# Loading `wq` as two 64-row transfers, one issued by SyncE and one by ScalarE

## The chip, the cores and the metric

The kernel runs on one core of a Trainium2 chip. The metric is the device time of one execution in microseconds. The kernel before took 680.11 us (median of three runs, 680.04 to 680.23). One execution was profiled; numbers of instructions, transfers and waits below come from it.

## The reference

Eight batch rows of one decode step: a layer norm of `x`, grouped-query attention over a cached K and V of 4096 positions, and a gated MLP whose SiLU gates the attention output. Cut to what matters:

```python
# x [8,1,512], k_cache and v_cache [8,8,4096,128], wq [512,4096], wo [4096,512]
xn = layernorm(x)
q = (xn @ wq) as [8, 32 heads, 1, 128]            # 4 query heads share one of the 8 KV heads
p = softmax(q @ k^T * 128**-0.5);  o = p @ v
s = o as [8,1,4096] @ wo
z = gelu(xn @ w_in); z1, z2 = halves of 896; z2 = layernorm(z2)
g = silu((z1 * (w_sp * z2 + b_sp)) @ w_out)
out = x + s * g
```

All data are float32. K and V are 134.2 MB each, so nearly all of the bytes are the cache.

## The kernel before, in words

Everything that is large is staged through a ring of three SBUF slots (`ring`, line 68; `slot()`, line 75). A slot has 128 rows (partitions) of 16384 float32, that is 64 KB a row and 8.39 MB in all. The loads go round the ring in program order, and each is issued by SyncE with one `dma_start` of 128 rows:

- slot 0: `wq` (line 80), the weight of the query projection, laid out as 4 blocks of 4096 columns a row;
- slot 1: `mlp_slot`, which holds `x` (line 96; 8 rows of 2 KB), `w_mlp` (line 97; 128 rows of 39 KB: `w_in`, most of `w_out`, the side constants) and the four `w_ex` pieces (line 101; rows of `w_out` that are fetched separately to 12 or 20 rows). The first `w_ex` waits for a memset by GpSimd (line 99);
- slots 2, 0, 1, 2, 0, 1, ...: for each of the 8 KV heads two halves of K (`load_k`, line 318) and two halves of V (`load_v`, line 323), 32 loads of 8.39 MB;
- after the last of them, `wo` in six pieces (line 365) in one more slot, and `x_rows` (line 367).

So the second K half of head 0 goes into the slot that `wq` had, and the first V half into the slot of the MLP weights. A load is issued when its slot has been read for the last time; SyncE's queue is in order, so a load that waits holds up all loads behind it.

Besides the slot, a load waits for the semaphore on which it will tell of its landing: there are eight of them for DMAs, taken in turn by all loads in program order. The load that takes a semaphore a second time waits until the load that had it eight places before has landed.

The compute of the head of the kernel runs in this order: the layer norm (lines 145 to 149, 8 rows of VectorE work and a power on GpSimd), its transpose `xnT` (line 152), two query projections of 32 matmul records each (`project_q`, line 247, which read `wq_sb`), and the MLP (`mlp()`, lines 157 to 240), whose last reads of the MLP slot are the matmuls of lines 223 and 227. Then, head after head, `scores` (line 267), `softmax` (lines 270 to 296) and `values` (line 303). At the end `project_o` (line 341) and `direct` (line 386) multiply by `wo`, two VectorE operations (lines 404 and 405) apply the gate and add `x`, and ScalarE issues the store (line 406).

ScalarE otherwise has little to do: its first instruction in the kernel before is the table load for the `Tanh` of the MLP (line 178).

Of the kernel before, what the change touches and what calls it, by code (L numbers as in the profile page):

```python
# [13 lines left out]
P = 128  # L14
# [46 lines left out]
def tile_gqa_gmlp_decode(ctx: ExitStack, tc: tile.TileContext, x, kT, v, wq, wo, w_mlp, w_ex0, w_ex1, w_ex2, w_ex3, x_rows, out, gate, stored):  # L61
    nc = tc.nc
# [12 lines left out]
    def slot():  # L75
        return ring.tile([P, SLOT], F32, name="slot")


    wq_sb = slot()
    nc.sync.dma_start(wq_sb, wq)  # L80
    wq_sb = wq_sb.rearrange("p (k n) -> p k n", k=NK)
    mlp_slot = slot()
    n_in, n_out = NK * 2 * FH, (NB - MOVED) * D
# [376 lines left out]
```

## Time and profile before

| | |
|---|---|
| median of 3 runs | 680.11 us |
| the profiled execution | 680.09 us |
| its span, first to last instruction | 678.5 us |
| mean granted clock of TensorE | 0.748 |
| TensorE matmul busy | 342.9 us (51% of the span) |
| VectorE / ScalarE / GpSimd busy | 81.2 / 13.8 / 7.9 us |
| read from HBM | 290.78 MB, 429 GB/s over the span |

How to read it: the page gives the busy time of each engine, then the span in 40 equal slices with a digit for the busy share in tenths, the mean share of the 16 DMA engines and the GB/s that they moved. The chain of waits follows the work that ended last back from the last instruction. A name such as "SPq" is an engine's sequencer, which issues DMAs and waits; "PE" is TensorE, "DVE" VectorE, "ACT" ScalarE, "POOL" GpSimd, "SP" SyncE. A window's GB/s counts a DMA packet where it starts; in this kernel a packet is one row of a transfer.

### The profile page before, as it was taken

To read this page: it belongs to the slowest core of one execution; us is meant where nothing else is said; L and a number is where in the kernel's file an instruction comes from. 1 tells how busy PE (TensorE), PEld (TensorE's weight loads), DVE (VectorE), ACT (ScalarE), POOL (GpSimd) and SP (SyncE) were. 2 spreads that over 40 slices of the span, in tenths; PEclk is the share of its full clock that TensorE was granted. 3 is DMA by queue.
4 is the path that set the end of the run, shared out by engine and by line. 5 is a ranking of instruction groups with operands and counts; after the bars stand their busy time and mean duration, and the time that the engine had idled before them with its cause. 6 is when DMAs were issued, how large, how long until landed. Compare 5 with 4: busy or idle time off the path is not lost.

```text
span 678.5 us, 5312 instructions
## 1 busy us (share of the span) xinstructions
PE 342.9 (51%) x2465; PEld 94.4 (14%) x2465; DVE 81.2 (12%) x155; ACT 13.8 (2%) x28; POOL 7.9 (1%) x17
## 2 busy tenths in 40 slices
PE   0448744346555444555553444555544346555547
PEld 0112211111111111111111011111111011111103
DVE  1143021102100021101101021101111021100211
ACT  0010000000000000000000000000000000000000
POOL 3000000000000000000000000000000000000000
PEclk9987856787766678787666778777656777876669
DMA  9999999999999999999999999999999999999997
GB/s 379 458 440 430 430 433 430 433 430 433 430 437 430 433 433 430 437 430 437 434 433 441 440 433 430 433 430 440 434 437 430 433 433 430 430 437 437 434 428 300
DMA packets 6165, 291.15 MB, mean 429 GB/s; under 512 B 952, under 2 KB 1080, under 8 KB 1496
## 3 DMA queue, kind: packets, MB, share of 16 engines
q1 hardware_dynamic: 6000, 290.79, 99.2%
q8 instruction: 19, 0.31, 0.2%
q10 hardware_dynamic: 144, 0.03, 0.0%
q14 instruction: 2, 0.02, 0.0%
HBM read 290.78 MB, written 0.03 MB: 429 GB/s over the span
## 4 chain that ended last, share of the span: by engine, by line
DMA 78%; PE 16%; issue 4%; DVE 0%; SPq 0%; POOLq 0%; POOL 0%
DMA slot<-in_kT 35%; DMA slot<-in_v 33%; PE sc L267 7%; PE o_ps L303 7%; DMA slot<-in_wo 7%; DMA slot<-in_x 3%; PE scr L223 1%; PE scr L227 1%; SPq L365 0%; PE acc L386 0%; PE scr L216 0%; DVE st L145 0%; POOLq L454 0%; POOL rstd L148 0%; PE scr L205 0%
## 5 line engine op out<-in xcount | busy, mean ns | idle before, releaser
L267 PE MATMUL sc<-slot,qz 128*32 128x512 f32 x1024 | 146.2, 735 | 129.9 <-DMA slot<-in_kT 129.9
L303 PE MATMUL o_ps<-slot,pT 128*16 128x512 f32 x1024 | 147.6, 741 | 112.1 <-DMA slot<-in_v 112.1
L267 PEld LDWEIGHTS sc<-slot,qz 128*32 128x32 f32 x1024 | 38.3, 132 | 231.2 <-issue 149.6
L303 PEld LDWEIGHTS o_ps<-slot,pT 128*16 128x16 f32 x1024 | 32.9, 113 | 213.6 <-issue 151.2
L272 DVE TENSOR_REDUCE nm<-sc 128x1 f32<-128x1024 f32 x8 | 9.8, 1225 | 273.2 <-PE sc L267 273.2
L306 DVE TENSOR_TENSOR o_all<-o_ps,diag 128x512 f32<-128x512 f32 x16 | 11.1, 692 | 245.9 <-PE o_ps L303 245.9
L313 PE MATMUL po_ps<-fold,o_sb 128*128 128x16 f32 x32 | 6.4, 276 | 28.4 <-DVE o_sb L308 28.4
L274 ACT ACTIVATE p<-sc,nm 128x1024 f32<-128x1024 f32 x8 | 8.9, 1113 | 551.6 <-DVE nm L272 551.6
L308 DVE TENSOR_REDUCE o_sb<-o_all 128x128 f32<-128x512 f32 x16 | 16.7, 1045 | 0.5
L152 PE MATMUL scr<-ident,slot 8*128 8x8 f32 x4 | 0.6, 254 | 25.1 <-DVE slot L149 25.1
L313 PEld LDWEIGHTS po_ps<-fold,o_sb 128*128 128x128 f32 x32 | 4.9, 190 | 42.7 <-DVE o_sb L308 42.3
L294 DVE STREAM_TRANSPOSE pT<-p 128x1024 f32<-128x1024 f32 x8 | 10.0, 1245 | 0.3
L247 PE MATMUL scr<-slot,xnT 128*32 128x512 f32 x64 | 9.2, 726 | 0.3 <-issue 0.3
L277 PE MATMUL scr<-ident,nm 128*1 128x128 f32 x8 | 2.2, 270 | 10.8 <-DVE nm L272 10.8
L290 PE MATMUL scr<-wl,same 128*128 128x1 f32 x16 | 3.8, 309 | 6.5 <-DVE wl L288 6.5
L292 DVE TENSOR_SCALAR p<-p,w,wl 128x1024 f32<-128x1024 f32 x8 | 6.5, 813 | 0.3
L341 PE MATMUL sc<-slot,oT 128*8 128x256 f32 x56 | 5.0, 380 | 1.6 <-DMA slot<-in_wo 1.6
L223 PE MATMUL scr<-slot,rest 128*32 128x512 f32 x10 | 5.5, 1057 | 0.0
L186 PE MATMUL scr<-part_sum,same 128*128 128x1 f32 x4 | 1.1, 347 | 8.4 <-DVE part_sum L184 8.4
L341 PE MATMUL o_ps<-slot,oT 128*8 128x256 f32 x56 | 4.8, 379 | 0.0
L290 PEld LDWEIGHTS scr<-wl,same 128*128 128x128 f32 x16 | 3.4, 265 | 7.0 <-PE scr L283 7.0
L283 PE MATMUL scr<-ident,full 1*128 1x1 f32 x8 | 1.8, 226 | 5.1 <-DVE full L281 5.1
(93 smaller groups left out, 69.5 us busy)
## 6 DMA issues: line engine op xcount, KB each, us to landing
slot<-in_w_mlp SPq DMA_DIRECT2D x1, 4880.0 KB, 32.6
slot<-in_wo SPq DMA_DIRECT2D x1, 4608.0 KB, 39.5
slot<-in_wo SPq DMA_DIRECT2D x1, 2048.0 KB, 44.0
slot<-in_wo SPq DMA_DIRECT2D x2, 512.0 KB, 44.8
slot<-in_wo SPq DMA_DIRECT2D x1, 384.0 KB
slot<-in_kT SPq DMA_DIRECT2D x16, 48.5
slot<-in_v SPq DMA_DIRECT2D x16, 48.3
slot<-in_w_ex SPq DMA_DIRECT2D x1, 240.0 KB
```

The costliest lines, as they stand in the source:

```text
L223: nc.tensor.matmul(pw[R * g:R * (g + 1), :], hT[:, a, R * g:R * (g + 1)], w_out_sb[:, i, :], start=(a == 0), stop=False)
L247: nc.tensor.matmul(pq[R * g:R * (g + 1), :], xnT[:, k, :], wq_sb[:, k, lo:lo + REP * DH], start=(k == 0), stop=(k == NK - 1))
L267: nc.tensor.matmul(sc[R * g:R * (g + 1), c, :], qz[:, h, b * R:(b + 1) * R], k_sb[:, i, c, g, :], start=(b == 0), stop=(b == B - 1))
L272: nc.vector.tensor_reduce(m, sc, op=ALU.max, axis=AX.XY, negate=True)
L274: nc.scalar.activation(p, sc.rearrange("p c s -> p (c s)"), AF.Exp, bias=m, accum_out=l[:, h:h + 1])
L290: nc.tensor.matmul(tot, same_all, wl, start=True, stop=True)
L294: nc.vector.transpose(pT.rearrange("p j b g r -> p j g b r"), p.rearrange("p (j g b r) -> p j g b r", j=J, g=G, b=B))
L303: nc.tensor.matmul(of[R * i:R * i + G * REP, :], pT[:, j, half * HALF + i], v_sb[:, i, j], start=(j == 0), stop=(j == J - 1))
L306: nc.vector.tensor_mul(o_all, o, diag[:, :, None].to_broadcast([P, G, DH]))
L308: nc.vector.tensor_reduce(o_sb, o_all.rearrange("p g d -> p d g"), op=ALU.add, axis=AX.X)
L313: nc.tensor.matmul(po[:, half * n:(half + 1) * n], o_sb, fold.rearrange("p i r -> p (i r)"), start=True, stop=True)
L341: mm = nc.tensor.matmul(part[i][R * q:R * q + B, :], oT[:, h, r, :], wo_sb[:, m, i * half_d:(i + 1) * half_d], start=(m < REP), stop=(m == ...
```

## The change

One line is replaced by two. Rows 0 to 63 of `wq` are loaded by SyncE, at the place in its queue where all 128 rows were; rows 64 to 127 are loaded by ScalarE, as the first DMA of its queue and its first instruction. The bytes, the source, the destination and the length of a row (64 KB) are the same.

```diff
     wq_sb = slot()
-    nc.sync.dma_start(wq_sb, wq)
+    nc.sync.dma_start(wq_sb[:P // 2], wq[:P // 2])
+    nc.scalar.dma_start(wq_sb[P // 2:], wq[P // 2:])
     wq_sb = wq_sb.rearrange("p (k n) -> p k n", k=NK)
```

There is one DMA more, so every later load takes the next semaphore of the eight. Lines of the changed kernel from the second `dma_start` on have numbers higher by one.

In the instruction streams as built, the order on every engine is otherwise as before. The first matmul of `project_q` waits for the semaphores of both halves. The first K load, which waited for nothing before, is now the ninth DMA and waits for the semaphore of SyncE's half of `wq`; the second K load waits for that of ScalarE's half and for TensorE, where before it waited for that of the whole `wq` and for TensorE.

## The prediction

> **What bounds the kernel now.** I read the page's slices first, then the queues, then the chain of waits.
>
> ```profile
> span 678.5 us, 5312 instructions
> DMA  9999999999999999999999999999999999999997
> GB/s 379 458 440 430 430 433 430 433 430 433 430 437 430 433 433 430 437 430 437 434 433 441 440 433 430 433 430 440 434 437 430 433 433 430 430 437 437 434 428 300
> ...
> q1 hardware_dynamic: 6000, 290.79, 99.2%
> ...
> DMA 78%; PE 16%; issue 4%; DVE 0%; SPq 0%; POOLq 0%; POOL 0%
> ```
>
> The DMA engines are busy in every slice, at 430 to 440 GB/s; one queue, SyncE's, carries 290.79 MB; 78% of the chain is DMA. The rest of the chain is matmuls, so the question is whether any transfer waits for them. In the chain, in order of time (start, length, what):
>
> ```profile
> 1.16 21.61 DMA slot<-in_x
> ...
> 60.82 3.59 PE scr L227 x14
> ...
> 64.47 31.83 DMA slot<-in_v
> ...
> 96.43 9.65 PE o_ps L303 x64
> ...
> 106.09 48.11 DMA slot<-in_kT
> ...
> 570.00 47.85 DMA slot<-in_kT
> ...
> 630.03 44.75 DMA slot<-in_wo
> ```
>
> A K load is issued at 106.09, when its slot is free, and lands 48.1 us later; the last K of the chain lands at 570.00 + 47.85 = 617.85. From the landing of the first V (64.47 + 31.83 = 96.30) to there lie 9 turns of the chain, each one turn of the three-slot ring, so 27 loads: 521.55 / 27 = 19.32 us a load, and 8.39 MB in 19.32 us is 434 GB/s. A load that takes 48 us to land after its issue therefore stands behind about 29 us of other transfers: the queue never runs dry, and the ten microseconds of matmuls in the chain delay nothing. The windows by stage say the same (stretch, length, busy time of each engine, TensorE clock, DMA share, GB/s):
>
> ```profile
> 0.00:23.00 23.00, 0.00 (x0) 0.00 (x0) 2.09 (x8) 0.00 (x0) 6.75 (x15) 1.00 0.94 393
> 23.00:35.00 12.00, 8.75 (x60) 2.99 (x64) 2.49 (x7) 0.00 (x0) 0.54 (x1) 1.00 1.02 443
> ...
> 96.00:640.00 544.00, 274.75 (x1864) 71.83 (x1868) 55.48 (x91) 9.85 (x21) 0.00 (x0) 0.72 1.00 434
> ```
>
> So the time is one stream of DMAs, plus a start of under 2 us and a tail. A microsecond that the stream loses anywhere is a microsecond of the kernel, and one that compute gains in the head is worth nothing.
>
> **The head.** SyncE's issues, the first work of ScalarE, and how the compute stands to them:
>
> ```profile
> 0.73 0.37 SPq L80 DMA_DIRECT2D slot<-in_wq  x1
> 1.16 0.35 SPq L96 DMA_DIRECT2D slot<-in_x  x1
> 1.55 0.35 SPq L97 DMA_DIRECT2D slot<-in_w_mlp  x1
> 3.98 3.25 SPq L101 DMA_DIRECT2D slot<-in_w_ex  x4
> 7.27 29.73 SPq L318 DMA_DIRECT2D slot<-in_kT  x2
> 64.47 8.39 SPq L323 DMA_DIRECT2D slot<-in_v  x2
> ...
> 44.53 1.28 ACT L178 ACT_TABLE_LOAD   x1 [44.53 <-DVE zu L177]
> ```
>
> ```profile
> 22.79 0.68 DVE L145 BATCH_NORM_STATS2 st<-slot 8x6 f32<-8x512 f32 x1 [17.68 <-DMA slot<-in_x]
> ...
> 26.02 5.55 PE L247 MATMUL scr<-slot,xnT 128*32 128x512 f32 x32 [0.33 <-issue]
> ...
> 77.03 5.34 PE L267 MATMUL sc<-slot,qz 128*32 128x512 f32 x32 [4.54 <-DMA slot<-in_kT]
> ...
> slot<-in_w_mlp SPq DMA_DIRECT2D x1, 4880.0 KB, 32.6
> slot<-in_wq SPq DMA_DIRECT2D x1, 21.9
> ```
>
> `wq` lands at 0.73 + 21.9 = 22.6, `x` right behind it, `w_mlp` at 1.55 + 32.6 = 34.2. The second K is issued at about 36.7, while the first K is under way, and lands just before 77.03; the first V is issued at 64.47, so at that moment the stream still has 12.5 us of work.
>
> **The change part by part.** *Issue.* SyncE's issue of 64 rows is bounded by nothing and by the 0.37 us that it took for 128; the two issues behind it keep their places. ScalarE's new issue is priced at the same 0.37 us and stands where ScalarE idles until 44.53; without that cover it would cost 0.37 us once. If both sequencers share what makes the packets, the stream might start up to 0.37 us later or earlier: plus or minus 0.4, taken as 0.
>
> *Waits.* TensorE's first `project_q` matmul waits for two semaphores instead of one; the row at 26.02 shows 0.33 us of idling there, which bounds it, and it lies off the stream: 0. The first K load, issued at 7.27 before, now waits until SyncE's half of `wq` has landed. Behind it on SyncE wait the second K and the first V, and TensorE waits for those. What covers it are the transfers of `w_mlp` and `w_ex`, which stand behind that half in SyncE's own queue: 34.2 - 22.6 = 11.6 us for `w_mlp` alone, against an issue of 0.37 and a start of under 1 us (1.16 to the first rows at 1.50 to 2.25, below). Cost 0, with some 10 us to spare; with no cover it would be a hole of about 1.5 us.
>
> *The transfer.* The bytes and the rows stay, so a fair sharing of the 16 engines costs nothing. That is the lower end: 0. The upper end comes from how the engines move rows now (windows of 0.75 us, with the empty stretches between them):
>
> ```profile
> 1.50:2.25 0.75, 0.00 (x0) 0.00 (x0) 0.48 (x1) 0.00 (x0) 0.75 (x1) 1.00 4.25 1398
> 2.25:4.50 2.25, 0.00 (x0) 0.00 (x0) 0.18 (x1) 0.00 (x0) 2.21 (x5) 1.00 0.00 0
> ...
> 14.25:15.00 0.75, 0.00 (x0) 0.00 (x0) 0.00 (x0) 0.00 (x0) 0.00 (x0) 1.00 3.22 1398
> 15.00:16.75 1.75, 0.00 (x0) 0.00 (x0) 0.00 (x0) 0.00 (x0) 0.00 (x0) 1.00 0.00 0
> 16.75:17.50 0.75, 0.00 (x0) 0.00 (x0) 0.00 (x0) 0.00 (x0) 0.00 (x0) 1.00 3.23 1398
> 17.50:19.25 1.75, 0.00 (x0) 0.00 (x0) 0.00 (x0) 0.00 (x0) 0.00 (x0) 1.00 0.00 0
> 19.25:20.00 0.75, 0.00 (x0) 0.00 (x0) 0.00 (x0) 0.00 (x0) 0.00 (x0) 1.00 3.23 1398
> ```
>
> 1398 GB/s in 0.75 us is 1.05 MB, exactly sixteen rows of 65,536 bytes: each engine starts one row, then none starts for 1.75 us, then sixteen again. The engines take whole rows, one at a time, and march in step; a step is 19.32 / 8 = 2.42 us. Now let the ways into SBUF belong to the rows rather than to the engines. With 128 rows in one transfer each engine has eight rows and a way of its own. With 64 rows spread over the same 16 engines, the engines would stand two to a way. Each row then takes two steps, 4.83 us. The other queue's half uses the other ways, but because the engines march in step and take the queues in turn, all would write low rows, then all high rows, and half of the ways would idle at any moment. Each half takes what a whole slot takes now: 2 x 19.32 = 38.64 instead of 19.32, a loss of 19.3 us.
>
> No row of this trace has two engines on one way, or 64 rows, so the price lies between 0 and 19.3. I take the side of the upper end, since the windows show the lockstep that it needs: a steady 434 GB/s with all engines starting within 0.75 us after eight rows says that nothing shuffles them apart. A pair that is offset by some time saves that offset at each of the 7 row changes. Sixteen starts fit in 0.75 us at every step, so an offset within a pair is between 0 and 0.75, a saving of 0 to 5.3; I take 0.2 us, 1.4 in all, as the starts must fill the window between them and a pair is two of sixteen. The loss is then 19.3 - 1.4 = 17.9 us.
>
> [...]
>
> *What is late next.* `wq` and, behind it or with it, `x` and `w_mlp` land 17.9 us later, and so do `project_q`, the MLP and the issue of the first V, each relative to a stream that is itself 17.9 later. The 12.5 us of slack at the first V stays. Nothing further is lost, and nothing made up: from there on every transfer has 128 rows again.
>
> *The sum*, against the profiled execution's 680.09 us (span 678.5, 1.6 around it; 0.02 under the median): issue 0, waits 0, transfer +17.9: 698.0 us.
>
> **The rivals.**
>
> *No clash: the halves only share the engines* (not slower). The two queues' rows mix freely, or the ways can take two engines' rows at full pace; 8.39 MB still take 19.32 us, and the time is 680.1, between 679.7 and 680.5 by the 0.4 of the issue. For it: the stream runs at 434 GB/s with rows of 39 KB and of 64 KB alike, as if the engines were the limit. Against it: the lockstep. It decides from the point where paired engines are half the time on different halves. [...]
>
> *Part of a clash.* The two issues reach the engines in different order, so some pairs start out of step, or the pairs drift by half a row: 8 x 1.2 us saved of 19.3, about +9.7, so 689.8, anywhere from 682 to 695. Against it: the slowest pair sets the landing of a load, and a pair in step pays in full.
>
> *Faster by an early `x`.* `x` stands behind 64 rows instead of 128 in SyncE's queue. If it landed early, the 26.02 - 22.76 = 3.3 us from `x` to the first projection would be done before `wq` lands, the MLP would end 3.3 us earlier, and the time would be 676.8. Its place is the first V load, its point a stream that is empty at 64.47; with 12.5 us of work left there it does not decide.
>
> *The first K's new wait opens a hole.* If SyncE's half landed after `w_mlp` had passed, the stream would idle; both stand in one queue, so this needs engines far apart. It adds about 1.5 to 4 us to the forecast: 700 to 702.
>
> **How the numbers follow.** Forecast, both halves clash in step: 0.71. Part of a clash: 0.10. No clash: 0.13. Early `x`: 0.02. A hole besides: 0.04. The forecast's own range goes from 19.3 - 5.3 = 14.0 to 19.3 and 0.4 of issue: 694 to 700. To hold 8 in 10 the range reaches down into the part of a clash, to 686, and up to the hole, to 702; outside it lie no clash, early `x` and the lower end of the part. About 0.2% (1.4 us) is what a measurement of this kernel can tell from no change. Slower by more than that: 0.71 + 0.10 + 0.04 = 0.85. Within it: 0.12, the case without a clash. Faster: 0.03, early `x` and a rest.
>
> **What would show it.** In the changed profile, the windows from 1.5 to 40 us should show 16 rows starting every 4.8 us or 210 to 235 GB/s, the first slices near half of 434, and `wq` landing at 39 to 42 us, with 434 GB/s again from there and all later landings 17.9 us late. The first K should be issued when SyncE's half lands, with no hole after it. If the first slices still show 379 and 458 GB/s and the second K lands near 77, there is no clash. If `wq` is on time and the end is late, my reading of the stream is wrong.

## The result, and the profile after

The changed kernel takes 700.27 us (median of five runs, 699.96 to 700.53) against 680.11 us: slower by 20.16 us, a ratio of 1.0297 with a 95% interval of 1.0285 to 1.0309. The forecast was 698.0, its range 686 to 702. The page of the changed kernel, span, slices, queues and two landings:

```profile
span 698.8 us, 5314 instructions
...
DMA  9899999999999999999999999999999999999997
GB/s 240 180 345 422 436 451 428 425 431 451 420 432 431 444 428 425 446 431 432 424 447 435 429 431 440 431 432 435 428 432 435 447 425 424 432 461 424 418 421 313
...
q1 hardware_dynamic: 5936, 286.59, 96.3%
q10 hardware_dynamic: 224, 4.23, 2.8%
...
slot<-in_w_mlp SPq DMA_DIRECT2D x1, 4880.0 KB, 52.3
```

The DMA engines count as busy from the first slice on, as before, but in the first two slices they move 240 and 180 GB/s where they moved 379 and 458. ScalarE's queue (q10) now carries 4.23 MB: its half of `wq`, and the store. `w_mlp` lands 52.3 us after its issue, not 32.6. Windows over the head and over the long middle:

```profile
0.00:40.00 40.00, 0.00 (x0) 0.00 (x0) 1.88 (x7) 0.00 (x0) 6.75 (x15) 1.00 0.98 210
...
116.00:660.00 544.00, 274.24 (x1860) 71.61 (x1864) 55.48 (x91) 9.85 (x21) 0.00 (x0) 0.72 1.00 434
```

210 GB/s for 40 us is 8.4 MB, which is `wq` and nothing else; afterwards the stream runs at the same 434 GB/s as before. So the whole loss lies in the one load that was cut in two. Narrow windows show its rows:

```profile
1.50:2.05 0.55, 0.00 (x0) 0.00 (x0) 0.48 (x1) 0.00 (x0) 0.55 (x1) 1.00 0.00 0
...
6.60:6.70 0.10, 0.00 (x0) 0.00 (x0) 0.00 (x0) 0.00 (x0) 0.10 (x2) 1.00 3.08 655
6.70:7.60 0.90, 0.00 (x0) 0.00 (x0) 0.00 (x0) 0.00 (x0) 0.62 (x3) 1.00 5.12 1092
...
36.10:36.20 0.10, 0.00 (x0) 0.00 (x0) 0.00 (x0) 0.00 (x0) 0.00 (x0) 1.00 3.08 655
36.20:37.10 0.90, 0.00 (x0) 0.00 (x0) 0.00 (x0) 0.00 (x0) 0.00 (x0) 1.00 5.13 1092
```

655 GB/s in 0.10 us is one row of 65,536 bytes, 1092 in 0.90 us is fifteen more: again sixteen rows to a step. Six steps lie between 6.6 and 36.1, so a step takes 29.5 / 6 = 4.92 us where it took 2.42. The queue's row of two such steps (packets, MB) tells which rows they were; first 6.5 to 8 us, then 11.5 to 13 us:

```profile
q1 hardware_dynamic: 16, 1.05, 327.9%
...
q10 hardware_dynamic: 16, 1.05, 328.1%
```

Sixteen rows of SyncE's half, then sixteen of ScalarE's: here the engines take the two queues in turn, a row at a time. The share is that of sixteen engines over 1.5 us, so each of the sixteen rows took 3.279 x 1.5 = 4.92 us, the whole step. The waits moved as a block. Two of SyncE's issues, by time, and then the first V in the chain of waits:

```profile
0.73 0.59 SPq L80 DMA_DIRECT2D slot<-in_wq  x1
...
42.89 14.51 SPq L319 DMA_DIRECT2D slot<-in_kT  x2
```

```profile
84.80 31.78 DMA slot<-in_v
```

The first K, which now waits for SyncE's half, is issued at 42.89 instead of 7.27, and the first V at 84.80 instead of 64.47. The first V lands at 84.80 + 31.78 = 116.58, 20.28 us later than the 96.30 of before. That is the loss of `wq` and nothing more, so the new wait opened no hole.

### The profile page after: what moved, and what is told of

Read it like the earlier page. It is cut to its first block, busy times and chain, and to the rows that moved or that the text cites. A ratio compares the mean times of both kernels' runs of the same rounds, so it can differ in the third digit from the quotient of the medians.

```text
span 698.8 us, 5314 instructions
## 1 busy us (share of the span) xinstructions
PE 342.7 (49%) x2465; PEld 94.4 (14%) x2465; DVE 81.2 (12%) x155; ACT 13.8 (2%) x28; POOL 7.9 (1%) x17
## 3 DMA queue, kind: packets, MB, share of 16 engines
q10 hardware_dynamic: 224, 4.23, 2.8%
## 4 chain that ended last, share of the span: by engine, by line
DMA 79%; PE 16%; issue 4%; DVE 0%; SPq 0%; POOLq 0%; POOL 0%
DMA slot<-in_kT 34%; DMA slot<-in_v 32%; PE sc L268 7%; PE o_ps L304 7%; DMA slot<-in_wo 6%; DMA slot<-in_x 6%; PE scr L224 1%; PE scr L228 1%; SPq L366 0%; PE acc L387 0%; PE scr L217 0%; DVE st L146 0%; POOLq L455 0%; SPq L80 0%; POOL rstd L149 0%
## 6 DMA issues: line engine op xcount, KB each, us to landing
slot<-in_w_mlp SPq DMA_DIRECT2D x1, 4880.0 KB, 52.3
slot<-in_wo SPq DMA_DIRECT2D x1, 4608.0 KB, 39.4
```

## The experiments

Each was timed beside the kernel before on the same chip; that took 680.01 to 680.14 us in the batches. Four questions were asked: is it the second queue, is it the rows, is it SBUF or HBM, and does it hang on the lockstep. A further run moves the whole `wq` to ScalarE.

**Both halves by SyncE.**

```diff
-    nc.scalar.dma_start(wq_sb[P // 2:], wq[P // 2:])
+    nc.sync.dma_start(wq_sb[P // 2:], wq[P // 2:])
```

> Both 64-row halves are issued by SyncE, one behind the other, so there is one queue. Theory 'ways' (the ways into SBUF belong to the rows, and 64 rows put two engines on each way): all engines write low rows for four steps and high rows for four, each step 4.92 us as in the changed kernel, so wq takes 39.4 us and the time is 699.5 to 700.5. Rival 'two queues' (the loss comes from engines switching between the queues of two issuers): one queue, so 680.1, at most 0.4 more for the added issue.

Measured: 701.40 us (701.23 to 701.63), ratio 1.0313 (1.0298 to 1.0329). One queue loses as much as two, so the second issuer is not the cause. The time is 0.9 above the range and 1.1 slower than the changed kernel: here two 64-row transfers one behind the other were a little slower still than two in turn. Why was not found.

**Halves by columns.**

```diff
-    nc.sync.dma_start(wq_sb[:P // 2], wq[:P // 2])
-    nc.scalar.dma_start(wq_sb[P // 2:], wq[P // 2:])
+    nc.sync.dma_start(wq_sb[:, :SLOT // 2], wq[:, :SLOT // 2])
+    nc.scalar.dma_start(wq_sb[:, SLOT // 2:], wq[:, SLOT // 2:])
```

> Two transfers again, one by SyncE and one by ScalarE, of the same bytes, but each has all 128 rows and half of the columns (rows of 32 KB). Theory 'ways': every engine has its own way in both, so 680.1, between 679.7 and 680.6. Rival 'two queues': the engines still switch between two queues, so about 700. Rival 'one more transfer costs 20 us': about 700.

Measured: 680.06 us (679.88 to 680.14), ratio 0.9999 (0.9990 to 1.0008). Two queues, two issuers, one more transfer and the first K's new wait are all in this kernel, and together they cost nothing. Its first 20 us:

```profile
0.00:20.00 20.00, 0.00 (x0) 0.00 (x0) 1.88 (x7) 0.00 (x0) 6.75 (x15) 1.00 0.94 393
```

393 GB/s including the start, against the changed kernel's 210, and from 20 to 40 us it is 434: with 128 rows in each transfer, two queues cost no pace.

**Four transfers of 32 rows, eight of 16**, all by SyncE (32 becomes 16 in the second kernel):

```diff
-    nc.sync.dma_start(wq_sb[:P // 2], wq[:P // 2])
-    nc.scalar.dma_start(wq_sb[P // 2:], wq[P // 2:])
+    for r in range(0, P, 32):
+        nc.sync.dma_start(wq_sb[r:r + 32], wq[r:r + 32])
```

> wq in four transfers of 32 rows, all by SyncE. [...] Rival 'each more transfer costs 20 us': three more, so about 740. Rival 'no way is shared below some number of rows': 680.1. [...]

> wq in eight transfers of 16 rows, all by SyncE; each engine gets one row of each. [...] Rival 'a narrow transfer runs at half rate, however narrow': 700. Rival 'each more transfer costs 20 us': seven more, so about 820.

Measured: 701.04 us (700.99 to 701.25) with 32 rows and 734.97 us (733.59 to 735.33) with 16, ratio 1.0803 (1.0787 to 1.0819). All of the rivals' times are far off. So 32 neighbouring rows are as slow as 64, although there are four transfers: 210 GB/s over the first 20 us, as in the changed kernel over 40. With 16 rows it is about half of that pace. The eight transfers of 16 rows, in a window in which nothing else moves:

```profile
5.00:69.00 64.00, 0.00 (x0) 0.00 (x0) 0.11 (x2) 0.00 (x0) 2.32 (x6) 1.00 1.03 115
```

115 GB/s is slightly over a quarter of 434 (108). At that pace the 8.39 MB of `wq` take 73 us, an estimate, against 19.32 before: 53.7 of the 54.9 us by which this kernel is slower. The cost follows which rows a transfer takes, not the number of transfers.

**Even and odd rows.**

```diff
-    nc.sync.dma_start(wq_sb[:P // 2], wq[:P // 2])
-    nc.scalar.dma_start(wq_sb[P // 2:], wq[P // 2:])
+    nc.sync.dma_start(wq_sb[0::2], wq[0::2])
+    nc.scalar.dma_start(wq_sb[1::2], wq[1::2])
```

> SyncE loads the even rows of wq and ScalarE the odd ones, 64 rows each, so each transfer touches low and high rows. [...] Rival 'low against high half' (the loss comes from a transfer that lies in one half of the rows): both halves are touched at any time, 680.1.

Measured: 680.41 us (680.24 to 680.77), ratio 1.0004 (0.9994 to 1.0013): full pace with 64 rows. The rival held. A transfer of 64 rows is not slow in itself (680.41 us); it is slow when its rows are neighbours in one half (700.27). Windows of its first steps:

```profile
5.00:6.00 1.00, 0.00 (x0) 0.00 (x0) 0.12 (x2) 0.00 (x0) 1.00 (x1) 1.00 2.42 1049
6.00:7.50 1.50, 0.00 (x0) 0.00 (x0) 0.00 (x0) 0.00 (x0) 1.32 (x6) 1.00 0.00 0
7.50:8.25 0.75, 0.00 (x0) 0.00 (x0) 0.00 (x0) 0.00 (x0) 0.00 (x0) 1.00 3.23 1398
```

1049 GB/s in 1 us and 1398 in 0.75 us are sixteen rows each; the next sixteen start some 2.4 us later, as with 128 rows, not 4.92.

**Source or destination.** So far the rows in HBM and in SBUF were the same ones. Two kernels part them, with `wq` laid out in HBM to suit, so that the same data reach the same place. First low rows from a spread source, then spread rows from half of the source; each pair of lines stands in place of the two issues of the changed kernel:

```diff
+    nc.sync.dma_start(wq_sb[:P // 2], wq[0::2])
+    nc.scalar.dma_start(wq_sb[P // 2:], wq[1::2])
...
+    nc.sync.dma_start(wq_sb[0::2], wq[:P // 2])
+    nc.scalar.dma_start(wq_sb[1::2], wq[P // 2:])
```

> As the changed kernel on the side of SBUF (SyncE fills rows 0 to 63, ScalarE rows 64 to 127), but wq lies in HBM with the two halves of rows interleaved, so each transfer reads every second row of the source. If the loss comes from where the rows go in SBUF: 699.5 to 702. If it comes from where they lie in HBM (a source of one contiguous half): 680.1 to 680.8, as with even and odd rows.

> The opposite pairing: SyncE fills the even rows of SBUF and ScalarE the odd rows, each from one contiguous half of the source in HBM, where the even rows lie ahead of the odd ones. If the loss comes from SBUF: 680.1 to 680.8. If it comes from HBM: 699.5 to 702.

Measured: 699.99 us (699.75 to 700.33), ratio 1.0293 (1.0278 to 1.0308), and 680.47 us (680.25 to 680.98), ratio 1.0006 (0.9997 to 1.0016). The loss goes with the rows of SBUF and not with those of the source.

**Is it the lockstep?** My forecast had low and high rows each using half of the ways at different times, because the engines are in step. `x` uses 8 engines: as it and `wq` end, between 20 and 22.5 us, the kernel before has 24 packets under 512 bytes, 16 for `wq` and 8 for `x`. Put into SyncE's queue between two pieces of SyncE's half, it should break the step.

```diff
+    nc.sync.dma_start(wq_sb[:P // 2, :2048], wq[:P // 2, :2048])
+    nc.scalar.dma_start(wq_sb[P // 2:, :2048], wq[P // 2:, :2048])
...
     nc.sync.dma_start(x_sb, x)
+    nc.sync.dma_start(wq_sb[:P // 2, 2048:], wq[:P // 2, 2048:])
+    nc.scalar.dma_start(wq_sb[P // 2:, 2048:], wq[P // 2:, 2048:])
```

In the control, `x` stands behind both pieces. In a third kernel `x` is read in two runs a row, from a source padded to 264 columns a run; in a fourth only 5 rows stand between, and the other 3 behind:

```diff
-    nc.sync.dma_start(x_sb, x)
+    nc.sync.dma_start(x_sb.rearrange("p (a f) -> p a f", a=2), x[:, :, :D // 2])
...
-    nc.sync.dma_start(x_sb, x)
+    nc.sync.dma_start(x_sb[:5], x[:5])
```

> The changed kernel with each 64-row half cut by columns into a first piece (8 KB a row) and the rest (56 KB a row), SyncE's half and ScalarE's alike; x stands behind both pieces, as in the changed kernel. It is the control of the next two. Theory 'ways and step': the engines stay in step, wq takes as long as in the changed kernel, 699.5 to 701. Theory 'half rate' (a 64-row transfer is slow by itself, step or no step): the same.

> Only x (8 rows of 2 KB, one row on each of 8 engines) is moved: in SyncE's queue it stands between the two pieces of its half. Theory 'ways and step': on 8 of the 16 engines x and its landing mark take two turns of SyncE's queue, while their partners already take a long low row, so partners are for some turns on different halves. Counting turns of a 56 KB row at full pace (2.15 us), the control needs 16 (eight rows, all doubled); here two of the eight are not doubled, 14, so 4.3 us less than the control: 695 to 697. Theory 'half rate': no change against the control, 700.

> As x between, with x read as two runs of 1 KB a row (its source is padded), so that x and its landing mark take three turns on those 8 engines instead of two. Theory 'ways and step': the same count gives 12 turns instead of 16 if ScalarE's rows come first at each engine, 8.6 us less than the control, 691 to 693, and some 12 us less, 688, if SyncE's come first. Theory 'half rate': 700.

> As x between the pieces, but only 5 of its 8 rows stand there (one row on each of 5 engines); the other 3 are loaded behind. With all 8 the time did not fall, though eight engines were on low rows and eight on high rows at once: so the engines that meet on a way stand together among the eight that x uses, or among the other eight. Five is odd, so at least one pair is split now. Theory 'step' (a way serves one engine at full pace while its partner is on the other half): in some turns 2 rows of 56 KB, or 6 if partners are four apart, pass in about 2.15 us, seen in the windows as row starts between the sixteen-row steps; the other pairs still set the time, 699.5 to 701. Theory 'no step' (a 64-row transfer is slow in itself): sixteen rows start in each step and none between, and the time is 699.5 to 701 too.

Measured: control 699.81 us (699.60 to 700.22), `x` between 700.36 (700.11 to 700.46), in two runs 700.73 (700.48 to 700.93), five rows 700.25 (699.90 to 700.36). Nothing was won, where the theory "step" had forecast 695 to 697 with `x` between and 688 to 693 in two runs. Yet the step was broken. In the kernel with `x` between, the queues' rows for 10.5 to 12 us (packets, MB), and the windows around:

```profile
q1 hardware_dynamic: 16, 0.48, 148.9%
q10 hardware_dynamic: 8, 0.46, 143.0%
```

```profile
10.50:12.00 1.50, 0.00 (x0) 0.00 (x0) 0.00 (x0) 0.00 (x0) 0.00 (x0) 1.00 2.92 623
12.00:15.00 3.00, 0.00 (x0) 0.00 (x0) 0.00 (x0) 0.00 (x0) 0.00 (x0) 1.00 0.00 0
15.00:16.50 1.50, 0.00 (x0) 0.00 (x0) 0.00 (x0) 0.00 (x0) 0.00 (x0) 1.00 2.96 612
```

q1 has the 8 small rows of `x` and 8 low rows of 56 KB (0.46 of its 0.48 MB), q10 has 8 high rows. So eight engines write low rows and eight high rows at once, and still none starts another row until after 15.0: all sixteen take over 4 us a row, where 56 KB at full pace would take 2.42 x 56 / 64 = 2.1. With five rows of `x` it is five high rows beside eleven low ones, and the windows have no row start in between either:

```profile
q1 hardware_dynamic: 16, 0.64, 240.7%
q10 hardware_dynamic: 5, 0.29, 107.3%
```

```profile
10.50:11.75 1.25, 0.00 (x0) 0.00 (x0) 0.00 (x0) 0.00 (x0) 0.00 (x0) 1.00 3.48 742
11.75:14.90 3.15, 0.00 (x0) 0.00 (x0) 0.00 (x0) 0.00 (x0) 0.00 (x0) 1.00 0.00 0
```

Of q1's 16 packets 5 are `x` and 11 are low rows, 0.63 of its 0.64 MB. If each way served a lone engine at full pace, some of these sixteen rows would have passed in half the time. The theory "step" is refuted in that form.

**The whole `wq` by ScalarE**, an edit of the kernel before:

```diff
-    nc.sync.dma_start(wq_sb, wq)
+    nc.scalar.dma_start(wq_sb, wq)
```

> The whole wq, 128 rows, is issued by ScalarE; SyncE starts with x and w_mlp, whose rows the engines now take in turn with those of wq. Theory 'one stream': x lands some 20 us earlier and wq some 10 us later (eight pairs of a 2.42 us and a 1.44 us row, 31 us from the start), the projections and the issue of the first V come 6 to 8 us later, still before the second K has landed at 77, so all of it is hidden and the time is 680.1, between 679.6 and 680.6. Rival 'ScalarE's queue is the slow part': 690 or more. Rival 'the head is not covered': 686 to 690.

Measured: 682.45 us (680.48 to 683.22 in nine runs), ratio 1.0032 (1.0021 to 1.0042). The head went as said: the first projection waits for `wq` until 32.90, and the first V is issued at 71.06 (the first matmuls of TensorE, then the chain of waits):

```profile
32.90 6.50 PE L247 MATMUL scr<-slot,xnT 128*32 128x512 f32 x32 [24.60 <-DMA slot<-in_wq]
```

```profile
71.06 25.52 DMA slot<-in_v
```

So nearly seven more microseconds of compute delay in the head did not show as such, and both rivals are far off in size. But the median is 1.9 us above the range, and the runs scatter over 2.7 us where the kernel before scatters over 0.3.

The profiled run, one of the quicker ones at 681.16 us, shows where its part begins: the stream runs short at the first V. Packets from 71.9 to 72.5 us, in the kernel before and then here (a packet under 512 bytes is read as the mark with which an engine ends its share of a load: in the kernel before there are 16 of them from 60 to 78 us, where one load, the second K, ends):

```profile
DMA packets 19, 0.61 MB, mean 1010 GB/s; under 512 B 9, under 2 KB 9, under 8 KB 9
...
DMA packets 15, 0.33 MB, mean 546 GB/s; under 512 B 10, under 2 KB 10, under 8 KB 10
```

Nine engines before and ten here end the second K in this stretch. Before, nine rows follow at once (0.59 MB of SyncE's queue); here only five (0.33 MB), for the first V was issued at 71.06, just 0.8 us ahead of the stretch. Windows over the next microseconds, before and here:

```profile
72.00:76.00 4.00, 0.50 (x8) 0.00 (x0) 0.00 (x0) 0.00 (x0) 0.00 (x0) 1.00 1.01 430
...
72.00:76.00 4.00, 4.00 (x56) 1.64 (x51) 1.20 (x4) 0.26 (x1) 0.00 (x0) 1.00 0.98 344
```

86 GB/s less for 4 us is 0.34 MB, an estimate of 0.8 us at 434 GB/s. The first V lands at 71.06 + 25.52 = 96.58, only 0.28 us late, but the last `wo` is late by 1.20 (675.98 against 674.78), about as much as the run is slower:

```profile
628.74 47.24 DMA slot<-in_wo
```

So the rival "the head is not covered" has a small part of the mechanism right. Why the loss shows only at the end, and why other runs take up to 683.22 us, was not found.

## Why the prediction was right, and where it was not

*One stream bounds the kernel:* right. The first V landed 20.28 us late, the end came 20.16 us late, and the 434 GB/s between them did not change.

*Issue, waits:* right in effect for this change. Halves by columns have the extra issue, the extra semaphore and the first K's new wait, and stand 0.05 us from the kernel before. The two issues did take longer, 0.59 us for SyncE's against 0.37, and no row starts before 2.05, where before sixteen start between 1.50 and 2.25: a few tenths, which I had put at 0. The slack of 12.5 us at the first V was misread: it is that of the last engine to finish the second K. Nine engines are through with it by 72.5 us (the packets above), so for them it was 7.4 to 8 us. In the changed kernel the first V and the loads ahead of it are late together, so nothing came of it; with the whole `wq` on ScalarE something did.

*Rows to a way, 19.3 us:* the size of the term was right, and the engines did march in step, sixteen low rows and then sixteen high ones. A step takes 4.92 us instead of 2.42; eight steps are 39.4 us against 19.3, 20.0 more. The runs add what the trace before could not show: it hangs on the SBUF rows (699.99 with a spread source, 680.47 with spread rows), and 32 rows are no slower than 64. The picture behind the term, two engines to a way, was my supposition, and no run shows ways, nor which engines would share one; what the runs show is the step of 4.92 us. In the kernel with five rows between, where by the picture at least one pair was split, no row passed faster, and 64 rows do not double the step when they are every second one (680.41). So the doubling is right for neighbouring rows, but that a picture which fails elsewhere gave it is in part luck.

*The lockstep as the reason, and the saving of 1.4 us by offsets in a pair:* wrong, and this is the step that failed. The saving rested on the lockstep as the reason why the other half of the supposed ways would idle. Engines pulled out of step gained nothing in three kernels. Without that term the sum would be 680.09 + 19.3 = 699.4; the remaining 0.9 up to 700.27 is the step's 4.92 instead of 4.83 (8 x 0.09 = 0.7) and the later start.

*The rivals:* no clash at 680.1 is refuted for neighbouring rows and is just what even and odd rows do. Part of a clash did not happen. The early `x` did not even arrive early: it took its turn behind the rows of both halves, and landed just before 43.27, when the layer norm began:

```profile
43.27 0.68 DVE L146 BATCH_NORM_STATS2 st<-slot 8x6 f32<-8x512 f32 x1 [38.16 <-DMA slot<-in_x]
```

The hole at the first K did not open.

*What stays open:* which rows each engine takes in a 64-row transfer, and why a row stays slow when half of the engines write to the other half, although even rows, which lie in both halves, pass at full pace (680.41 us).

## What to carry to other kernels

When DMA bounds a kernel, look at which SBUF rows a transfer writes before at who issues it: a cut by columns over two queues cost nothing here (680.06 us against 680.11), a cut into two halves of neighbouring rows doubled the time of the load (39.4 us against 19.3), and pieces of sixteen rows nearly quadrupled it (73 us, an estimate from 115 GB/s). If 64 rows must go alone, spread ones (every second row) kept the full pace here (680.41 us). Slack that is read from the landing of a load is that of its slowest engine: the others can be idle sooner, here by up to 5 us. A DMA share of 0.98 does not mean full pace: the engines counted as busy at 210 GB/s, and only the GB/s told.

## What the runs showed of the hardware that was not expected

Even rows alone passed at the pace of all 128 rows (680.41 us), so the pace is not a matter of the number of rows. Eight engines on low and eight on high rows at once were no faster than sixteen on one half: over 4 us for each 56 KB row, where the 4.92 us of a 64 KB row on one half make 4.3. And with 16 rows to a transfer the engines together reached 115 GB/s, a little more than a quarter of 434. The sixteen engines do not end a load together: of the second K, in the kernel before, nine were through by 72.5 us, and it landed only just before 77.03.
